# Passes 2 and 3 of a gated feed-forward: parting an odd chunk's activations beside the next chunk, and spreading the down weights' sums and loads over steps

## The chip, the cores and the metric

The kernel runs on one core of one Trainium2 chip. The metric is the device time of one launch in microseconds (us), as the median of several runs. The engines are named as in the profile: PE (TensorE, matmuls), PEld (its weight loads), ACT (ScalarE), DVE (VectorE), POOL (GpSimd), and SP, which here issues the DMAs. Each engine works through its own queue in order; semaphores tie the queues together.

## The reference

One transformer block in fp32 over 2048 tokens of width 1024, with a modulation (shift, scale, gate) computed from a condition vector `c`:

```python
x = A_x
sa, ca, ga, sb, cb, gb = silu(c) @ w_mod          # six rows of 1024
h = layernorm(x) * (1 + ca) + sa
x = x + ga * infini_attention(h)                  # 32 heads, 4 segments, with wq, wk, wv, wo
h = layernorm(x) * (1 + cb) + sb
x = x + gb * ((gelu(h @ w_gate) * (h @ w_up)) @ w_down)   # F = 3584
```

The change touches only the last line, the feed-forward.

## The kernel before

The attention and its projections come first (to about 1190 us of the profile). The feed-forward then runs in three passes over the tokens: 768, 640 and 640 of them (`PASSES`). Each pass walks over the 28 chunks of 128 columns of `w_gate`/`w_up` (`fc`; `m` counts chunks through all passes, so pass 2 begins at m = 28 and pass 3 at m = 56). The passes take the stretches 1190 to 1840, 1840 to 2415 and 2415 to 3012 us of the profile, roughly.

**Precision.** Each fp32 operand is parted into a high part (fp32r) and the rest: `cut`, or the local `put`, is one ACT copy for the high part (`nc.scalar.activation(hi, src, AF.Copy)`, L777 or L1082) and one subtraction for the low part (L779 on DVE for the down weights, L1083 on DVE for activations). Each product is three matmuls, hi·hi, lo·hi and hi·lo.

**One chunk** (`gate_up`, L1011 on) computes gate and up products with a seven-product (Winograd-Strassen) scheme. Seven products, in the order 1, 6, 2, 7, 5, 4, 3, go into three PSUM tiles `pa`, `pb`, `pc` (tile `f` in the profile, 12 matmuls each, all L1022). After product 1 ACT copies `pa` to `c1` (L1034, tile `c`); product 2 then goes on accumulating in `pa`, so it has to wait for this copy. After product 6 DVE forms `u2 = pb + c1` (L1036); product 7 then accumulates in `pb` and has to wait for that. Then come `g1 = gelu(pa)` (ACT L1038), two sums for `u3` (DVE L1040, L1042), `g2 = pb + c1` (DVE L1044), `g2 = gelu(g2)` (ACT L1045), and at the end `u2 += pc`, `g1 *= u2`, `g2 *= u3` (DVE L1047, L1048, L1049). The two results of a chunk are the tile `g`, of which there are two buffers.

**The down product** of passes 2 and 3 takes two chunks at a time, an even m and m + 1 (`down_seven`, matmuls L1148 into tiles `da`, `db`, `ds`, `dc`, `dd`). It is a seven-product scheme again, so it needs sums of both operands:

- `hidden(m)` makes the left operands (tile `hc`, three buffers). For an even chunk it parts `e1` and `e1 - e2`; for an odd chunk it needs sums with the even chunk before (`f`), and makes four parts: 512, 512, 256 and 128 columns wide. An odd chunk's `hidden` runs at the end of its `gate_up`; an even chunk's (but the first of a pass) is put into `delayed` and runs within the next `down_seven`, after the products `ds`.
- `t_part(m)` makes four of the right operands: it loads two raw chunks of `w_down` (tile `rt`, DMA at L1112), forms four differences on POOL (L790, two instructions of 256 columns each), and parts each into a tile `T` (ACT L777, DVE L779).
- `wd_load(m)` loads a chunk of `w_down` that pass 1 parted and stored in DRAM (tile `wd`, two buffers, 1 MB, DMA at L1010).

`gate_up`'s weights (tile `B`, eight buffers) are also loaded parted, seven products ahead (`b_load`, L978).

**The order.** PE's and SP's queues are in program order. For ACT, DVE and POOL a scheduler chooses the order from priorities; instructions handed to `keep` stay in program order among each other. `step()` is called after every half product, so 14 times in a chunk; it lets each generator in `sides` go on to its next `yield`. `flush` runs generators of a kind to their end.

The chunks of a pass follow each other as gate_up(odd m+1), gate_up(even m+2), down_seven(m), gate_up(odd m+3), and so on: from the second pair on, one period of the pass is two `gate_up` and one `down_seven`. The last two chunks of a pass (26 and 27) use a plain down product (`down`, L1211). The output of the pass is scaled and added to the residual beside the next pass (`finish`, L1284 and L1285).

## Time and profile before

| | us |
|---|---|
| median of 3 runs (lowest, highest) | 3024.54 (3022.23, 3025.67) |
| the profiled execution: its time | 3013.8 |
| the profiled execution: span from first to last instruction | 3012.1 |
| busy: PE / PEld | 2861.3 / 2551.1 |
| busy: DVE / ACT / POOL | 1884.0 / 1269.9 / 892.6 |
| mean granted TensorE clock | 0.983 |

The profiled execution was 10.7 us quicker than the median, so sums are made against 3013.8. The page gives busy times, a row per group of instructions and the chain of work that ended last; the trace also gives stretches of time ("windows"), the order of instructions in time with the idle time ahead of each and what ended it ("timeline"), and totals of who waited for whom ("waits"). An idle engine costs nothing unless PE, which is busy 95% of the span, waits for it.

### The profile page before, as it was taken

The page shows a single profiled execution, that of the slowest core. Times are in us where ns is not written, and L with a number is a line of the kernel's source. Part 1 is how long each engine was busy: PE and PEld are TensorE (multiplying, and loading weights), DVE is VectorE, ACT ScalarE, POOL GpSimd, SP SyncE. Part 2 cuts the span into 40 slices and gives each one's busy share as a digit, 9 for nine tenths or more (in the row PEclk, how much of TensorE's full clock was granted, in tenths as well). Part 3 has the DMA queues.
Part 4 walks back from the last instruction along what each step waited for, and adds up shares of the span by engine and source line. Part 5 has one row for each costly group of instructions (what it writes and reads, how often), then busy time and mean ns, then how long its engine had stood idle before and what let it go on. Part 6 is the DMA issues. An engine that isn't in the chain of part 4 may idle for free.

```text
span 3012.1 us, 48791 instructions
## 1 busy us (share of the span) xinstructions
PE 2861.3 (95%) x17248; PEld 2551.1 (85%) x17248; DVE 1884.0 (63%) x4289; ACT 1269.9 (42%) x3108; POOL 892.6 (30%) x1420
## 2 busy tenths in 40 slices
PE   6999999999999999999999999999999999999997
PEld 4788887888888778999999898888888888888987
DVE  7565657667567535666666667556556666556556
ACT  5777766766666443545323333211212231122111
POOL 0333334333334424534555441101111001111100
PEclk8999999999999999999999999999999999999999
DMA  7566657675556566888798887866777797777665
GB/s 238 102 137 140 143 107 139 148 134 113 109 103 133 151 213 222 320 321 308 280 357 304 293 307 286 345 246 249 263 267 264 252 346 263 262 259 272 250 243 192
DMA packets 233429, 684.02 MB, mean 227 GB/s; under 512 B 23392, under 2 KB 60256, under 8 KB 222432
## 3 DMA queue, kind: packets, MB, share of 16 engines
q1 hardware_dynamic: 233184, 680.90, 71.0%
q8 instruction: 136, 2.23, 0.3%
q14 instruction: 109, 0.89, 0.1%
HBM read 455.36 MB, written 175.11 MB: 209 GB/s over the span
## 4 chain that ended last, share of the span: by engine, by line
PE 61%; DVE 11%; DMA 11%; POOL 6%; ACT 5%; issue 5%; SPq 1%; DVEq 0%; POOLq 0%; ACTq 0%
PE f L1022 20%; PE kv L366 9%; PE d L1211 6%; DMA rt<-wd 5%; PE y L627 4%; PE q L372 3%; POOL rt L790 3%; PE T L557 3%; PE db L1148 2%; PE da L1148 2%; PE ds L1148 2%; PE dc L1148 2%; PE S L493 2%; PE O L566 2%; DVE T L779 1%
## 5 line engine op out<-in xcount | busy, mean ns | idle before, releaser
L1022 PE MATMUL f<-A,B 128*128 128x320 f32 (+1 forms) x7056 | 1149.4, 323 | 75.9 <-ACT c L1034 53.6
L1022 PEld LDWEIGHTS f<-A,B 128*128 128x128 f32 x7056 | 1126.0, 192 | 94.6 <-ACT c L1034 60.4
L495 DVE CUSTOM_DVE_ANT_0 sj<-S,mask 128x384 f32<-128x384 f32 (+3 forms) x512 | 229.6, 487 | 227.1 <-PE S L493 208.7
L790 POOL TENSOR_TENSOR rt<-rt 128x256 f32<-128x256 f32 x104 | 78.4, 774 | 948.4 <-DMA rt<-wd 882.8
L497 ACT ACTIVATE sj<-sj,mm 128x384 f32<-128x384 f32 (+3 forms) x512 | 281.4, 551 | 114.3 <-DVE mm L495 114.0
L560 POOL TENSOR_SCALAR_AFFINE_SELECT pt<-pt 128x128 f32<-128x128 f32 x512 | 170.8, 354 | 336.9 <-ACT pt L559 331.2
L1211 PE MATMUL d<-wd,hc 128*128 128x512 f32 x1128 | 259.8, 390 | 0.9 <-DVE hc L1074 0.7
L1211 PEld LDWEIGHTS d<-wd,hc 128*128 128x128 f32 x1128 | 211.1, 188 | 44.9 <-DVE hc L1074 1.0
L366 PE MATMUL kv<-w,hha 128*128 128x256 f32 x1024 | 206.7, 288 | 3.4 <-ACT hha L335 3.4
L366 PE MATMUL kv<-w,hhh 128*128 128x256 f32 x1024 | 201.6, 285 | 0.0
L559 ACT ACTIVATE pt<-T 128x256 f32<-128x256 f32 (+3 forms) x512 | 181.8, 457 | 37.3 <-PE T L557 33.4
L202 POOL TENSOR_TENSOR w<-r,w 128x256 fp32r<-128x256 f32 x180 | 133.3, 771 | 165.8 <-ACT w L197 165.8
L366 PEld LDWEIGHTS kv<-w,hha 128*128 128x128 f32 x1024 | 169.1, 194 | 4.7 <-ACT hha L335 4.3
L1082 ACT ACTIVATE hc<-g 128x256 fp32r<-128x256 f32 (+2 forms) x182 | 72.8, 440 | 227.5 <-DVE acc L1157 124.0
L366 PEld LDWEIGHTS kv<-w,hhh 128*128 128x128 f32 x1024 | 166.3, 191 | 0.3 <-issue 0.2
L1246 DVE TENSOR_TENSOR acc<-acc,d 128x512 f32<-128x512 f32 x176 | 118.2, 684 | 57.7 <-PE d L1211 56.2
L366 PE MATMUL kv<-w,hla 128*128 128x256 f32 x512 | 147.2, 288 | 6.0 <-DVE hla L336 4.2
L557 PEld LDWEIGHTS T<-qs,ks 128*128 128x128 f32 x512 | 80.6, 189 | 85.3 <-issue 35.1
L557 PE MATMUL T<-qs,ks 128*128 128x256 f32 (+2 forms) x512 | 128.6, 360 | 20.0 <-DVE qs L510 7.5
L1040 DVE TENSOR_TENSOR c<-f,c 128x320 f32<-128x320 f32 (+1 forms) x84 | 43.0, 511 | 167.0 <-PE f L1022 167.0
L366 PE MATMUL kv<-w,hlh 128*128 128x256 f32 x512 | 145.0, 283 | 0.0
L1045 ACT ACTIVATE g<-g 128x320 f32<-128x320 f32 (+1 forms) x84 | 41.0, 488 | 237.4 <-DVE g L1044 237.4
(240 smaller groups left out, 5270.5 us busy)
## 6 DMA issues: line engine op xcount, KB each, us to landing
B<-bc_d SPq DMA_DIRECT2D x392, 512.0 KB, 5.6
bc_d<-B SPq DMA_DIRECT2D x196, 512.0 KB, 6.3
wd<-wc_d SPq DMA_DIRECT2D x56, 1024.0 KB, 4.8
wc_d<-wd SPq DMA_DIRECT2D x28, 1024.0 KB, 8.0
rt<-wd SPq DMA_DIRECT2D x52, 512.0 KB, 7.3
ks<-kh SPq DMA_DIRECT2D x64, 256.0 KB, 5.6
qs<-qh SPq DMA_DIRECT2D x64, 256.0 KB, 7.4
wm<-wmod SPq DMA_DIRECT2D x32, 512.0 KB, 5.4
```

What stands on the lines that cost most here:

```text
L202: eng.tensor_sub(w[:, 1, k:k + 256], r[:, k:k + 256], f32(w[:, 0, k:k + 256]))
L366: nc.tensor.matmul(ps, b[:, sl], w[:, a], start=(kt == 0 and a == 0 and b is hi), stop=(kt == KT - 1 and a == 1), **kw)
L495: nc.vector.tensor_tensor_reduce(out=sj[:, :nv], in0=ps[:, :nv], in1=mask[:, L - nv:], scale=-1.0, scalar=3.4e38, op0=ALU.add, op1=ALU.min ...
L497: nc.scalar.activation(sj[:, :nv], sj[:, :nv], AF.Exp, bias=mm[:, j, i:i + 1], scale=-1.0, accum_out=ll[:, i, j:j + 1])
L557: nc.tensor.matmul(ps[:, :nn], ks[:, j, kc * P:(kc + 1) * P], qs[:, j, L - nn:], start=True, stop=True)
L559: nc.scalar.activation(pt, ps[:, nn - n:nn], AF.Exp)
L560: nc.gpsimd.affine_select(pt[:, :P], pt[:, :P], pattern=[[1, P]], compare_op=ALU.is_ge, fill=0.0, base=0, channel_multiplier=-1)
L627: nc.tensor.matmul(ps, b[:, i * P:(i + 1) * P], w[:, a, g % 2], start=(g == 0 and a == 0 and b is hi), stop=(g == G - 1 and a == 1))
L790: nc.gpsimd.tensor_sub(dst[:, k], a[:, k], b[:, k])
L1022: nc.tensor.matmul(ps, B[m, i][:, a, kt * P:(kt + 1) * P], A[p, i, kt][b], start=(start and kt == 0 and a == 0 and b == 0), stop=(kt == 3 ...
L1148: nc.tensor.matmul(ps, t[:, c:c + P], B(a), start=(start and a == 0 and b == 0), stop=(stop and a == 1), skip_group_check=True)
L1211: nc.tensor.matmul(ps, hid[m][:, b, tt * P:(tt + 1) * P], down_w[m][:, a, nb * L:(nb + 1) * L], start=(m == chunks[0] and a == 0 and b == ...
```

## The change

Five edits, all in the feed-forward of passes 2 and 3.

1. An odd chunk's `hidden` is no longer run at the end of its `gate_up`. It becomes a generator in `sides` that waits three steps of the next (even) chunk and then makes its four parts on four steps; `down_seven` is preceded by `flush("ht")`. Its instructions are marked `keep`.
2. Its sums change places: `s2 = e2 - f1` goes to a temporary tile, `e2` and `e1` are overwritten, so that the even chunk's tile `f` is only read at the start. Counts and widths of the parts stay (512, 256, 512, 128 columns).
3. The tile `g` of a chunk is taken after product 2 has been issued, not at the chunk's start, since its buffer is now read during the chunk.
4. `t_part` becomes `pair_part`: loads of `rt` on steps 0 and 1, differences on steps 6, 8, 10, 12, partings on steps 9, 13, 15, 17 (before: loads on step 0, differences on 8, 12, 16, 20, partings on 11, 15, 19, 23), and the two `wd` loads on steps 11 and 19 instead of straight behind `down_seven`.
5. In `finish`, the multiplication by the gate is marked `keep` as well.

```diff
@@ -1028,13 +1028,13 @@
 
             pa, pb, pc = (s_ps(f"f{q}_{m}")[:, :h] for q in range(3))
             c1, u2, u3 = (c_tile(f"c{q}_{m}")[:, :h] for q in range(3))
-            feat[m] = ffp[3].tile([P, 2, HM], F32, name=f"g{m}", tag="g", bufs=2)
-            g1, g2 = (feat[m][:, q, :h] for q in range(2))
             product(pa, 1, True)
             nc.scalar.activation(c1, pa, AF.Copy)
             product(pb, 6, True)
             nc.vector.tensor_add(u2, pb, c1)
             product(pa, 2, False)
+            feat[m] = ffp[3].tile([P, 2, HM], F32, name=f"g{m}", tag="g", bufs=2)
+            g1, g2 = (feat[m][:, q, :h] for q in range(2))
             nc.scalar.activation(g1, pa, AF.Gelu_apprx_tanh)
             product(pb, 7, False)
             nc.vector.tensor_add(u3, pb, c1)
@@ -1049,11 +1049,22 @@
             nc.vector.tensor_mul(g2, g2, u3)
             if p > 0 and fc % 2 == 0 and fc > 0:
 
-                delayed.append(lambda: hidden(m))
+                delayed.append(lambda: run(hidden(m)))
+            elif seven(m) and fc % 2:
+
+                sides.append([chain(wait_for(3), hidden(m, True)), 1, "h"])
             else:
-                hidden(m)
-
-        def hidden(m):
+                run(hidden(m))
+
+        def run(gen):
+            for _ in gen:
+                pass
+
+        def wait_for(n):
+            for _ in range(n):
+                yield
+
+        def hidden(m, behind=False):
 
 
             p, fc = divmod(m, FC)
@@ -1072,6 +1083,7 @@
                         hi, lo = (v.rearrange("p (q t) -> p q t", q=2) for v in (hi, lo))
                     nc.scalar.activation(hi, src, AF.Copy)
                     nc.vector.tensor_sub(lo, src, f32(hi))
+                    yield
                 return
 
             def put(t, at, n, src, q=1):
@@ -1079,9 +1091,9 @@
                 hi, lo = t[:, at:at + n], t[:, at + n:at + 2 * n]
                 if q == 2:
                     hi, lo = (v.rearrange("p (q t) -> p q t", q=2) for v in (hi, lo))
-                nc.scalar.activation(hi, src, AF.Copy)
-                nc.vector.tensor_sub(lo, src, f32(hi))
-
+                held(nc.scalar.activation(hi, src, AF.Copy), nc.vector.tensor_sub(lo, src, f32(hi)))
+
+            held = keep if behind else lambda *ins: None
             w = 2 * P
             e1, e2 = g[:, 0, :w], g[:, 1, :w]
             t = place(0).rearrange("p a b -> p (a b)")
@@ -1094,36 +1106,49 @@
                 return
             z = place(1).rearrange("p a b -> p (a b)")
             f = feat[m - 1]
-            nc.vector.tensor_add(f[:, 1, :w], f[:, 1, :w], e2)
-            nc.vector.tensor_sub(f[:, 0, :w], e2, f[:, 0, :w])
+            s2 = tmp_tile(f"s2_{m}")[:, :w]
             put(t, 0, 2 * w, g[:, :, :w], 2)
-            put(z, 0, 2 * w, f[:, :, :w], 2)
-            nc.vector.tensor_sub(e1, e1, f[:, 0, :w])
-            put(z, 4 * w, w, e1)
+            held(nc.vector.tensor_sub(s2, e2, f[:, 0, :w]))
+            held(nc.vector.tensor_add(e2, f[:, 1, :w], e2))
+            held(nc.vector.tensor_sub(e1, e1, s2))
+            yield
+            put(z, 0, w, s2)
+            yield
+            put(z, 2 * w, 2 * w, g[:, :, :w], 2)
+            yield
             put(t, 4 * w, P, g[:, :, w:h], 2)
-            left[m] = {2: (t, 0, 2 * w), 4: (t, w, 2 * w), 6: (z, 0, 2 * w), 5: (z, w, 2 * w), 3: (z, 4 * w, w),
+            left[m] = {2: (t, 0, 2 * w), 4: (t, w, 2 * w), 6: (z, 0, w), 3: (z, 2 * w, 2 * w), 5: (z, 3 * w, 2 * w),
                        0: (t, 4 * w, P)}
 
-        def t_part(m):
+        def pair_part(m):
+
 
             r = []
-            for q in range(2):
+
+            def raw(q):
                 r.append(ra_tile(f"rt{m + q}"))
                 nc.sync.dma_start(r[q], wd[(m + q) % FC])
-            b11, b12, b21, b22 = (r[q][:, k:k + L] for q in range(2) for k in (0, L))
-            for _ in range(8):
-                yield
+
+            def block(i, j):
+                return r[i][:, j * L:(j + 1) * L]
 
             def put(i, src):
                 t = big.tile([P, 2, L], F32R, name=f"T{m}_{i}", tag="raw", bufs=4)
-                cut(t[:, 0], t[:, 1], src, nc.vector)
+                cut(t[:, 0], t[:, 1], src, nc.vector, behind=True)
                 right[m, i] = t
 
-            for i, dst, a, b in ((5, b11, b12, b11), (7, b12, b22, b12), (6, b22, b22, b11), (4, b21, b21, b22)):
-                diff(dst, a, b)
-                for _ in range(3):
-                    yield
-                put(i, dst)
+            at = {11: lambda: wd_load(m), 19: lambda: wd_load(m + 1)}
+            if seven(m):
+                at.update({0: lambda: raw(0), 1: lambda: raw(1),
+                           6: lambda: diff(block(0, 0), block(0, 1), block(0, 0)),
+                           8: lambda: diff(block(0, 1), block(1, 1), block(0, 1)),
+                           10: lambda: diff(block(1, 1), block(1, 1), block(0, 0)),
+                           12: lambda: diff(block(1, 0), block(1, 0), block(1, 1)),
+                           9: lambda: put(5, block(0, 0)), 13: lambda: put(7, block(0, 1)),
+                           15: lambda: put(6, block(1, 1)), 17: lambda: put(4, block(1, 0))})
+            for n in range(24):
+                if n in at:
+                    at[n]()
                 yield
 
         def down_seven(m):
@@ -1281,7 +1306,7 @@
                 residual(q + 2)
                 yield
                 t = a[tt][:, nb * L:(nb + 1) * L]
-                nc.vector.tensor_mul(t, t, gbb[:, nb * L:(nb + 1) * L])
+                keep(nc.vector.tensor_mul(t, t, gbb[:, nb * L:(nb + 1) * L]))
                 keep(nc.vector.tensor_add(t, t, res[q]))
                 if nb:
                     later(4, lambda tt=tt: move_rows(p, tt, a[tt], out, store=True))
@@ -1318,25 +1343,21 @@
                 pend.append(m)
                 if len(pend) == 3:
                     if p > 0:
+                        flush("ht")
                         down_seven(pend[0])
                     else:
                         down(pend[:2], False)
                     pend = pend[2:]
                     if p > 0:
-                        wd_load(m)
-                        wd_load(m + 1)
-                        if seven(m):
-                            sides.append([t_part(m), 1])
-                        else:
+                        sides.append([pair_part(m), 1, "t"])
+                        if not seven(m):
                             sides.append([spread(), 1, "e"])
-            flush("e")
+            flush("et")
             down(pend, True)
             flush("a")
             send(True)
             if p + 1 < len(PASSES):
-                wd_load((p + 1) * FC)
-                wd_load((p + 1) * FC + 1)
-                sides.append([t_part((p + 1) * FC), 1])
+                sides.append([pair_part((p + 1) * FC), 1, "t"])
                 sides.append([finish(p), 1])
         yield
```

The instructions are the same in number and kind, and PE's queue is the same row by row. What moves is shown at three places, for the pair whose odd chunk is m = 43 and whose next even chunk is m = 44. In the names, `c_43` is a chunk's c1, u2 or u3, `f_43` its PSUM tiles; `g` and `hc` are followed by a running number only.

ACT's queue from chunk 43's gelu(pa) to chunk 44's, before:

```order
L1038 ACTIVATE g_24329<-f_43_24323 128x320
L777 ACTIVATE T_5_24425<-rt_24338 128x512
L777 ACTIVATE T_7_24483<-rt_24338 128x512
L777 ACTIVATE T_6_24518<-rt_24340 128x512
L777 ACTIVATE T_4_24553<-rt_24340 128x512
L1045 ACTIVATE g_24329<-g_24329 128x320
L1082 ACTIVATE hc_0_24449<-g_24329 128x512
L1082 ACTIVATE hc_1_24450<-g_24109 128x512
L1082 ACTIVATE hc_0_24449<-g_24329 128x128
L1034 ACTIVATE c_44_24465<-f_44_24462 128x320
L1082 ACTIVATE hc_1_24450<-g_24329 128x256
L1038 ACTIVATE g_24468<-f_44_24462 128x320
```

and now:

```order
L1038 ACTIVATE g_24380<-f_43_24326 128x320
L777 ACTIVATE T_5_24415<-rt_24340 128x512
L1045 ACTIVATE g_24380<-g_24380 128x320
L777 ACTIVATE T_7_24455<-rt_24340 128x512
L777 ACTIVATE T_6_24481<-rt_24348 128x512
L1032 ACTIVATE c_44_24464<-f_44_24461 128x320
L777 ACTIVATE T_4_24499<-rt_24348 128x512
L1094 ACTIVATE hc_0_24502<-g_24380 128x512
L1094 ACTIVATE hc_1_24503<-s_43_24504 128x256
L1038 ACTIVATE g_24531<-f_44_24461 128x320
```

The copy c1 of chunk 44 (`c_44<-f_44`) stood behind four T parts and three of chunk 43's four `hc` parts; now it stands behind three T parts and no `hc` part.

DVE's queue from chunk 43's `g2 = pb + c1` to chunk 44's u2, before:

```order
L1044 TENSOR_TENSOR g_24329<-f_43_24324,c_43_24326 128x320
L779 TENSOR_TENSOR T_4_24553<-rt_24340,T_4_24553 128x512
L1049 TENSOR_TENSOR g_24329<-g_24329,c_43_24328 128x320
L1097 TENSOR_TENSOR g_24109<-g_24109,g_24329 128x256
L1047 TENSOR_TENSOR c_43_24327<-f_43_24325,c_43_24327 128x320
L1098 TENSOR_TENSOR g_24109<-g_24329,g_24109 128x256
L1048 TENSOR_TENSOR g_24329<-g_24329,c_43_24327 128x320
L1083 TENSOR_TENSOR hc_0_24449<-g_24329,hc_0_24449 128x512
L1083 TENSOR_TENSOR hc_1_24450<-g_24109,hc_1_24450 128x512
L1101 TENSOR_TENSOR g_24329<-g_24329,g_24109 128x256
L1083 TENSOR_TENSOR hc_0_24449<-g_24329,hc_0_24449 128x128
L1036 TENSOR_TENSOR c_44_24466<-f_44_24463,c_44_24465 128x320
```

and now:

```order
L1044 TENSOR_TENSOR g_24380<-f_43_24327,c_43_24329 128x320
L1049 TENSOR_TENSOR g_24380<-g_24380,c_43_24331 128x320
L779 TENSOR_TENSOR T_7_24455<-rt_24340,T_7_24455 128x512
L1047 TENSOR_TENSOR c_43_24330<-f_43_24328,c_43_24330 128x320
L779 TENSOR_TENSOR T_6_24481<-rt_24348,T_6_24481 128x512
L1048 TENSOR_TENSOR g_24380<-g_24380,c_43_24330 128x320
L779 TENSOR_TENSOR T_4_24499<-rt_24348,T_4_24499 128x512
L1094 TENSOR_TENSOR hc_0_24502<-g_24380,hc_0_24502 128x512
L1111 TENSOR_TENSOR s_43_24504<-g_24380,g_24171 128x256
L1034 TENSOR_TENSOR c_44_24465<-f_44_24462,c_44_24464 128x320
```

Chunk 44's u2 (`c_44<-f_44,c_44`) had the first sums and parts of chunk 43 ahead of it; now three T parts, the first `hc` part and `s2` stand between chunk 43's g2 and it, and the other sums and parts of chunk 43 follow it.

SP's queue from the B load behind which `down_seven` is issued, before:

```order
L978 DMA B_3_24214<-bc_d 128x1024
L1010 DMA wd_24319<-wc_d 128x2048
L1010 DMA wd_24321<-wc_d 128x2048
L978 DMA B_1_24330<-bc_d 128x1024
L1112 DMA rt_24338<-wd 128x1024
L1112 DMA rt_24340<-wd 128x1024
L978 DMA B_6_24349<-bc_d 128x1024
```

and now:

```order
L978 DMA B_3_24221<-bc_d 128x1024
L978 DMA B_1_24332<-bc_d 128x1024
L1130 DMA rt_24340<-wd 128x1024
L1130 DMA rt_24348<-wd 128x1024
L978 DMA B_6_24351<-bc_d 128x1024
L978 DMA B_2_24366<-bc_d 128x1024
L978 DMA B_7_24382<-bc_d 128x1024
L978 DMA B_5_24399<-bc_d 128x1024
L978 DMA B_4_24419<-bc_d 128x1024
L1010 DMA wd_24435<-wc_d 128x2048
L978 DMA B_3_24439<-bc_d 128x1024
```

The two `wd` loads stood ahead of the `rt` loads; now the `rt` loads come right behind one B load, the first `wd` load stands behind five more B loads, and the second one five places behind that. (The new kernel's line numbers are shifted by 2 or more: L1034 stands now for u2 and L1032 for c1, L1094 for the `hc` parts, L1130 for the `rt` loads.)

## The prediction

> **What bounds the kernel now.** First the page:

> ```profile
> span 3012.1 us, 48791 instructions
> PE 2861.3 (95%) x17248; PEld 2551.1 (85%) x17248; DVE 1884.0 (63%) x4289; ACT 1269.9 (42%) x3108; POOL 892.6 (30%) x1420
> ```

> PE sets the end, so what can be won is time in which PE idles or has a lower clock. The windows of the three passes show where:

> ```profile
> 1190.00:1840.00 650.00, 642.02 (x3411) 599.31 (x3410) 430.29 (x669) 265.33 (x515) 313.45 (x368) 1.00 0.83 304
> 1840.00:2415.00 575.00, 541.27 (x3121) 500.78 (x3120) 350.84 (x654) 122.39 (x266) 86.31 (x104) 0.98 0.75 275
> 2415.00:3012.00 597.00, 547.85 (x3145) 507.85 (x3143) 359.36 (x666) 117.10 (x253) 84.34 (x104) 0.96 0.72 260
> ```

> Columns: stretch, length, busy time (count) of PE, PEld, DVE, ACT, POOL, granted clock, DMA share, GB/s. Pass 1 has PE busy for 642 of 650 us at clock 1.00. Passes 2 and 3 leave it idle for 34 and 49 us, at 0.98 and 0.96. PE's group and its waits in 1840 to 3012 us say for whom:

> ```profile
> L1022 PE MATMUL f<-A,B 128*128 128x320 f32 x4704 | 732.8, 317 | 68.8 <-ACT c L1034 53.5 <-DMA B<-bc_d 6.1 <-DVE c L1036 5.3
> PE f L1022 <- ACT c L1034: 53.5, 24, 3.3
> PE f L1022 <- DVE c L1036: 5.3, 2, 2.7
> PE f L1022 <- DVE c L1042: 3.3, 6, 0.8
> ```

> Of 68.8 us, 53.5 are 24 waits for one instruction, c1 (ACT, L1034), which product 2 needs. One of them in the timelines of PE, ACT and DVE (start, duration, engine, line, operation, count, idle time before and its releaser):

> ```profile
> 2026.95 16.00 PE L1022 MATMUL f<-A,B 128*128 128x320 f32 x108
> 2045.23 9.06 PE L1022 MATMUL f<-A,B 128*128 128x320 f32 x60 [2.28 <-ACT c L1034]
> ```
> ```profile
> 2028.97 0.44 ACT L1034 ACTIVATE c<-f 128x320 f32<-128x320 f32 x1 [7.21 <-PE f L1022]
> 2042.98 0.48 DVE L1048 TENSOR_TENSOR g<-g,c 128x320 f32<-128x320 f32 x1
> 2043.50 1.35 ACT L1082 ACTIVATE hc<-g 128x512 fp32r<-128x512 f32 x3 [2.15 <-DVE g L1048]
> 2044.76 0.41 ACT L1034 ACTIVATE c<-f 128x320 f32<-128x320 f32 x1
> ```

> The 108 matmuls are the odd chunk's 84 and the even chunk's products 1 and 6. At 16.00/108 = 0.148 us each, a product takes 1.78 us. The odd chunk's c1 started 2.02 us after its first matmul. The even chunk's first matmul is at 2026.95 + 84 × 0.148 = 2039.4, so its c1 could have run from 2041.4 to 2041.9, 1.1 us before PE ended product 6 at 2042.95. It ran at 2044.76 instead, since three `hc` parts of the odd chunk stood ahead of it on ACT and waited for DVE's L1048.

> The stall has a second cost. The rest of the even chunk behind it is 60 matmuls in 23 of the 24 cases. The one above took 9.06 us, as did seven others; 15 took over 10.3. The first, a usual one and the last of these 15:

> ```profile
> 2004.19 10.40 PE L1022 MATMUL f<-A,B 128*128 128x320 f32 x60 [2.45 <-ACT c L1034]
> 2085.00 10.59 PE L1022 MATMUL f<-A,B 128*128 128x320 f32 x60 [2.35 <-ACT c L1034]
> 2948.90 10.60 PE L1022 MATMUL f<-A,B 128*128 128x320 f32 x60 [2.20 <-ACT c L1034]
> ```

> 10.59 - 9.06 = 1.53 us for the same matmuls: lower clock right after an idle gap, 15 × 1.53 = 23 us in all, which fits clocks of 0.98 and 0.96 beside pass 1's 1.00.

> **The change, part by part.**

> *Odd chunks' parts move (edits 1 and 2).* Counts and widths stay, so ACT and DVE have no more work. On ACT c1 of the even chunk stands ahead of every `hc` part, so this wait goes: minus 53.5 us, and minus 23 us of clock. What is late next is u2 (DVE, L1036), which product 7 needs. Its chain is worked out from these rows:

> ```profile
> 2039.92 0.63 ACT L777 ACTIVATE T<-rt 128x512 fp32r<-128x512 f32 x1 [0.77 <-POOL rt L790]
> 2040.36 0.48 DVE L1044 TENSOR_TENSOR g<-f,c 128x320 f32<-128x320 f32 x1
> 2040.76 0.68 DVE L779 TENSOR_TENSOR T<-rt,T 128x512 fp32r<-128x512 f32 x1
> 2040.88 0.47 ACT L1045 ACTIVATE g<-g 128x320 f32<-128x320 f32 x1 [0.32 <-DVE g L1044]
> 2041.38 0.49 DVE L1049 TENSOR_TENSOR g<-g,c 128x320 f32<-128x320 f32 x1
> 2042.65 0.42 DVE L1098 TENSOR_TENSOR g<-g,g 128x256 f32<-128x256 f32 x1
> 2044.16 1.29 DVE L1083 TENSOR_TENSOR hc<-g,hc 128x512 fp32r<-128x512 f32 x2 [0.70 <-ACT hc L1082]
> ```

> On the same clock: the odd chunk's product 4 ends after 72 matmuls, at 2037.6, so L1044 runs to 2038.2, the gelu to 2038.7, L1049 to 2039.2. T 7 on ACT to 2039.3, on DVE to 2040.0; L1047 (as L1044) to 2040.5; T 6 to 2041.2; L1048 to 2041.7. T 4 on ACT follows c1, 2041.9 to 2042.5, on DVE to 2043.2; the 512-wide `hc` part, half of 1.29, to 2043.8; `s2` (as L1098) to 2044.3; u2 to 2044.7. Product 7 is due at 2042.95 + 1.78 = 2044.7. Its cover is gone, then, but just so. Rows that follow each other overlap by some 0.08 us (2040.36 + 0.48 against 2040.76), which lowers the sum; a hand-over raises it. I take 0.1 us for 24 pairs, plus 2 us; bounds are 0 and, with T parts as slow as below, 1.7 us a pair. Six waits for L1042, which stood behind T parts, go: minus 3 us.

> *The tile g later (edit 3)* costs nothing unless gelu(pa) waits for the odd chunk's sums; ACT runs it some 0.4 us later, and PE does not need its PSUM tile again within the chunk.

> *rt, T and wd (edit 4).* SP stood in the `wd` loads before, POOL got `rt` late, and differences and T parts ran side by side:

> ```profile
> 2019.49 6.57 SPq L1010 DMA_DIRECT2D wd<-wc_d  x2
> 2026.64 1.11 SPq L1112 DMA_DIRECT2D rt<-wd  x2
> 2033.37 1.44 POOL L790 TENSOR_TENSOR rt<-rt 128x256 f32<-128x256 f32 x2 [34.51 <-DMA rt<-wd]
> 2034.76 3.73 POOL L790 TENSOR_TENSOR rt<-rt,rt 128x256 f32<-128x256 f32 x4
> 2038.45 1.44 POOL L790 TENSOR_TENSOR rt<-rt 128x256 f32<-128x256 f32 x2
> 2039.19 1.25 DVE L779 TENSOR_TENSOR T<-rt,T 128x512 fp32r<-128x512 f32 x1 [1.29 <-ACT T L777]
> ```

> Now nothing that waits for the down product stands ahead of `rt`. The B load before it can go once its buffer is free, at about the start of the down product (2014), so `rt` may come up to 12 us earlier, POOL is done by about 2029, and T parts cost DVE 0.68 us and not 1.25. The `wd` loads get B loads ahead of and behind them. Landing times, 1900 to 2400 us:

> ```profile
> wd<-wc_d SPq DMA_DIRECT2D x25, 1024.0 KB, 4.8
> rt<-wd SPq DMA_DIRECT2D x24, 512.0 KB, 7.3
> 2984.17 13.79 PE L1211 MATMUL d<-wd,hc 128*128 128x512 f32 x60
> ```

> The second `wd` load goes out when the even chunk's product 6 is done. Five products (8.9 us) and 15 matmuls of the down product (13.79/60 = 0.23 us each, 3.4 us) lie before its first use: 12 us of cover for 4.8. Only at the end of a pass is it short: the load for chunk 27 goes out with that chunk's last product, 1.8 us before `down`, whose first 18 matmuls (4.1 us) use the other chunk: 5.9 us for a landing of 4.8 to 7.3, so 0 to 1.4 us, twice; I take 2 us in all. For the start of a pass, where the order of `finish` changes too (edit 5), I take nothing, with 5 us either way, the size of the L1036 waits there.

> **Sum** against the profiled 3013.8: - 53.5 - 23 - 3 + 2 + 2 = - 75.5, so 2938. The median was 10.7 us above the profiled run; carried over, 2949.

> **The rivals.**

> *The wait moves to u2.* For it speaks that its cover is used up. If `rt` comes no earlier, three T parts cost 0.57 us more each, 1.7 us a pair. Half of that, 0.9 × 24 = 21 us, and a few low clocks, give 2970 to 2990.

> *The clock does not come back.* Eight of 23 stalls, of the same length, were followed by full clock, so the gap alone does not decide. If the low stretches have another cause, 23 us stay: 2972. Against it: every one of the 15 begins at a stall, and pass 1, with PE denser, ran at 1.00. [...]

> *POOL beside the down product.* With `rt` early, POOL's differences fall where DVE adds up the down products:

> ```profile
> 2022.36 0.68 DVE L1157 TENSOR_TENSOR acc<-acc,dc 128x512 f32<-128x512 f32 x1
> 2024.17 1.54 PE L1148 MATMUL dc<-wd,hc 128*128 128x512 f32 x6
> ```

> The second of the two tiles `dc` is read by 2023.0, and PE goes on in it three matmuls after 2024.17, at 2024.9: 1.9 us of slack. Ahead of that read DVE has four instructions of an even chunk's `hidden`. If each waits for one POOL instruction (1.44/2 = 0.72 us), that is 2.9 us, 1.0 us of stall in a pair, 24 us: 2973. [...]

> *Slower: POOL's differences come late.* T 4 waits for POOL's last difference, and T 4 (0.63 and 1.25), the `hc` part, `s2` and u2 follow it: 3.4 us. From the landing of `rt` to that difference it was 6.5 us (2033.4 to 2039.9). So u2 ends 9.9 us after the landing, and is due at 2044.7. A pair now loses 76.5/24 = 3.2 us, of which 1.0 is clock. From a stall of 2.2 us on, a landing at 2037, 3.7 us later than before, it is a loss; 1 us beyond, 24 us: 3049. Against it: SP has less ahead of `rt` than before. If the landing falls just at that point, or c1 waits behind T 6 as long as it did behind `hc`, the change does not do what it says and nothing moves: 3024.

> **How the numbers follow.** Forecast, 2935 to 2962: 0.66. Wait at u2: 0.12. Clock stays: 0.10. POOL beside the down product: 0.05. Nothing moves: 0.03. Slower: 0.04. A measurement of this kernel can tell about 0.2% (6 us) from no change, so faster 0.93, same 0.03, slower 0.04. The range begins at 2932: if the median's extra 10.7 us were clock lost at the other eight stalls (8 × 1.53 = 12 us), it goes too, and the start of a pass may give 5. It ends at 2980, so as to take in the rivals at 2972 and 2973 and half of the wait at u2.

> **What would show it.** In the changed profile the waits of PE for c1 should be gone from the 24 places, and 168 matmuls of a pair should run in one piece of some 25 us, followed by a down product. The clock of passes 2 and 3 should be 0.99 or more, their PE idle time together below 35 us instead of 83. POOL's wait for `rt` should end some 10 us earlier relative to the odd chunk's first matmul, and T parts on DVE should cost 0.68 us. A row "PE f <- DVE c" for u2 of over 10 us would be the first rival; PE waits at `dc` the third; waits for `wd` ahead of `down`, the price at the ends of passes. The prediction would be wrong outright if PE waited for T, `wd` or `rt` in every pair.

## The result, and the profile after

The changed kernel takes 2942.78 us (median of 4 runs, 2937.51 to 2944.91), the kernel before 3024.01 us (median of 4 runs). The ratio is 0.9729, with a 95% interval of 0.9712 to 0.9746. The forecast was 2949 us in a range of 2932 to 2980. The profiled execution took 2937.51 us against 3013.8, which is 76.3 us less; the sum of the prediction had 75.5 less.

The head of the page of the changed kernel:

```profile
span 2935.8 us, 48789 instructions
PE 2833.2 (97%) x17248; PEld 2530.0 (86%) x17248; DVE 1854.5 (63%) x4289; ACT 1259.7 (43%) x3108; POOL 869.4 (30%) x1420
```

PE went from 95% to 97% of a shorter span. Two sets of windows of the changed kernel follow, with the same columns as before (stretch, length, busy time and count of PE, PEld, DVE, ACT, POOL, clock, DMA share, GB/s): first passes 2 and 3, then their steady parts and the stretch between them.

```profile
1840.00:2380.00 540.00, 525.10 (x3112) 488.11 (x3111) 340.44 (x669) 122.54 (x279) 73.71 (x104) 0.99 0.80 300
2380.00:2936.00 556.00, 536.95 (x3168) 500.51 (x3166) 340.84 (x657) 107.99 (x243) 73.41 (x104) 0.98 0.74 274
```
```profile
1930.00:2350.00 420.00, 420.00 (x2496) 391.83 (x2495) 261.87 (x512) 83.48 (x190) 61.98 (x88) 1.00 0.75 282
2350.00:2440.00 90.00, 74.17 (x421) 68.81 (x420) 57.35 (x115) 23.40 (x56) 5.61 (x8) 0.91 0.82 302
2440.00:2860.00 420.00, 420.00 (x2497) 391.88 (x2496) 256.93 (x503) 88.28 (x199) 66.64 (x95) 1.00 0.76 284
```

Read the second set first. In the pairs PE is busy for 420.00 of 420 us at clock 1.00: nothing is left to win there by order. What is lost is lost between the passes, 2350 to 2440, where PE is busy for 74 of 90 us at a clock of 0.91. The group of the gate and up products and the waits of PE in 1840 to 2936 us name the rest:

```profile
L1022 PE MATMUL f<-A,B 128*128 128x320 f32 x4704 | 699.6, 310 | 11.5 <-DVE c L1034 5.6 <-DMA B<-bc_d 2.4 <-DVE c L1042 2.2
```
```profile
PE d L1236 <- DMA wd<-wc_d: 7.7, 1, 7.7
PE f L1022 <- DVE c L1034: 5.6, 2, 4.7
PE f L1022 <- DVE c L1042: 2.2, 1, 2.2
```

The 24 waits for c1 (53.5 us before) are gone, and no row for u2 (now L1034) has taken their place: its 5.6 us are two waits at the starts of the passes. The matmuls themselves shrank too, from 317 to 310 ns on average. A new row stands on top: `down` (now L1236) waited once for `wd`, for 7.7 us.

A pair in the timeline of PE of the changed kernel, with the start of the next one:

```profile
2018.09 24.80 PE L1022 MATMUL f<-A,B 128*128 128x320 f32 x168
2055.25 24.80 PE L1022 MATMUL f<-A,B 128*128 128x320 f32 x168
```

All 168 matmuls run in one piece, and a pair takes 37.16 us. Before, a pair had 108 and 60 matmuls with a gap between.

**Where the time went.** By start times in the two timelines of PE: from the first `da` of pass 2 to the start of the last odd chunk's products it was 500.8 us and is 459.1 us (-41.7). In pass 3 it was 503.5 and is 458.5 (-45.0). The start of pass 2 gives another 4.1. The stretch from the last odd chunk of pass 2 to the first `da` of pass 3 went from 73.0 to 84.6 (+11.6). Pass 2's gate and up products began 2.9 later (1850.15 against 1847.22); that start varies from run to run, between 1845.5 and 1856.9 in three executions of kernels that are the same up to there. Together: -41.7 - 45.0 - 4.1 + 11.6 + 2.9 = -76.3. So the pairs gave 86.7 us, more than the sum had for everything, and the end of pass 2 took some back.

Here is that end in the changed kernel, first SP's queue (L840 loads the next pass's activations, L1010 is `wd`), then PE:

```profile
2357.46 2.16 SPq L840 DMA_DIRECT2D ra<-mix_d  x2
...
2366.68 0.36 SPq L840 DMA_DIRECT2D ra<-mix_d  x1
2367.28 0.33 SPq L1010 DMA_DIRECT2D wd<-wc_d  x1
...
2369.07 0.32 SPq L1010 DMA_DIRECT2D wd<-wc_d  x1
```
```profile
2362.85 2.02 PE L1022 MATMUL f<-A,B 128*128 128x320 f32 x12 [1.19 <-DVE c L1040]
2367.11 2.03 PE L1022 MATMUL f<-A,B 128*128 128x320 f32 x12 [2.23 <-DVE c L1042]
2376.84 16.54 PE L1236 MATMUL d<-wd,hc 128*128 128x512 f32 x60 [7.71 <-DMA wd<-wc_d]
2393.22 17.76 PE L1022 MATMUL f<-A,B 128*128 128x320 f32 x120
2415.67 21.58 PE L1022 MATMUL f<-A,B 128*128 128x320 f32 x132 [4.70 <-DVE c L1034]
```

The two `wd` loads of the last pair stand on steps 11 and 19 now. That puts them in SP's queue behind the loads of the next pass's activations, which held it until 2367. They were issued at 2367.28 and 2369.07, when the last chunk's products were nearly done: the first one 14.75 us after that chunk's first matmul (2352.53), where in the pair shown above it goes out 9.36 us after it (2027.45 against 2018.09). And it landed only 9.5 us later, at 2376.8, beside other loads (DMA share 1.0). So `down` had to wait 7.71 us. It then ran its 60 matmuls in 16.54 us; the same 60 took 13.79 before. In the kernel before both loads had gone out ahead of those activations, straight behind the last `down_seven`:

```profile
2387.93 6.57 SPq L1010 DMA_DIRECT2D wd<-wc_d  x2
```

Pass 3 has no pass behind it, and there `down` followed without a wait.

### The profile page after: what moved, and what is told of

Its sections match the earlier page's. It is cut to its first block, busy times and chain, and to the rows that moved or that the text cites. A ratio compares the mean times of both kernels' runs of the same rounds, so it can differ in the third digit from the quotient of the medians.

```text
span 2935.8 us, 48789 instructions
## 1 busy us (share of the span) xinstructions
PE 2833.2 (97%) x17248; PEld 2530.0 (86%) x17248; DVE 1854.5 (63%) x4289; ACT 1259.7 (43%) x3108; POOL 869.4 (30%) x1420
## 4 chain that ended last, share of the span: by engine, by line
PE 76%; DVE 8%; DMA 6%; ACT 4%; issue 3%; POOL 3%; SPq 0%; DVEq 0%; POOLq 0%; ACTq 0%
PE f L1022 32%; PE kv L366 9%; PE d L1236 7%; PE y L627 4%; PE q L372 3%; PE T L557 3%; PE dc L1173 2%; PE db L1173 2%; PE ds L1173 2%; PE da L1173 2%; PE S L493 2%; PE O L566 2%; ACT sj L497 2%; PE dd L1173 1%; DVE qs L510 1%
## 5 line engine op out<-in xcount | busy, mean ns | idle before, releaser
L1022 PE MATMUL f<-A,B 128*128 128x320 f32 (+1 forms) x7056 | 1116.3, 318 | 17.9 <-DVE c L1034 11.1
L1022 PEld LDWEIGHTS f<-A,B 128*128 128x128 f32 x7056 | 1101.7, 188 | 27.8 <-DVE c L1034 14.5
L790 POOL TENSOR_TENSOR rt<-rt 128x256 f32<-128x256 f32 x104 | 75.7, 750 | 888.1 <-DMA rt<-wd 607.9
L1236 PE MATMUL d<-wd,hc 128*128 128x512 f32 x1128 | 262.6, 393 | 8.8 <-DMA wd<-wc_d 7.7
L1236 PEld LDWEIGHTS d<-wd,hc 128*128 128x128 f32 x1128 | 212.9, 189 | 53.7 <-DMA wd<-wc_d 8.0
L1045 ACT ACTIVATE g<-g 128x320 f32<-128x320 f32 (+1 forms) x84 | 41.1, 489 | 299.2 <-DVE g L1044 299.2
L1032 ACT ACTIVATE c<-f 128x320 f32<-128x320 f32 (+1 forms) x84 | 38.3, 456 | 268.7 <-PE f L1022 268.7
L1094 ACT ACTIVATE hc<-g 128x256 fp32r<-128x256 f32 (+1 forms) x156 | 64.5, 446 | 154.2 <-DVE acc L1182 124.0
## 6 DMA issues: line engine op xcount, KB each, us to landing
B<-bc_d SPq DMA_DIRECT2D x392, 512.0 KB, 6.8
bc_d<-B SPq DMA_DIRECT2D x196, 512.0 KB, 6.4
wd<-wc_d SPq DMA_DIRECT2D x56, 1024.0 KB, 8.3
wc_d<-wd SPq DMA_DIRECT2D x28, 1024.0 KB, 8.1
rt<-wd SPq DMA_DIRECT2D x52, 512.0 KB, 8.2
wm<-wmod SPq DMA_DIRECT2D x32, 512.0 KB, 5.4
```

The costliest lines, as they stand in the source:

```text
L1022: nc.tensor.matmul(ps, B[m, i][:, a, kt * P:(kt + 1) * P], A[p, i, kt][b], start=(start and kt == 0 and a == 0 and b == 0), stop=(kt == 3 ...
L1236: nc.tensor.matmul(ps, hid[m][:, b, tt * P:(tt + 1) * P], down_w[m][:, a, nb * L:(nb + 1) * L], start=(m == chunks[0] and a == 0 and b == ...
```

## The experiments

All runs are kernels on one core. Each batch has its own median of the kernel before: 3025.37 us for the first four, 3021.37 for the next four, 3023.6 for the last two.

**Edits 1 to 3 and 5 without edit 4.** The odd chunk's parts move, the loads and T parts stay as before (excerpt):

```diff
-sides.append([pair_part(m), 1, "t"])
+wd_load(m); wd_load(m + 1)
+if seven(m): sides.append([t_part(m), 1])
```

> Edits 1 to 3 and 5 alone; t_part and the wd loads as before. Theory (the wait for c1 behind the odd chunk's parts, and the clock it costs, are the whole gain): the waits of PE for c1 are gone, u2 comes some 0.2 to 0.3 us late in each of 24 pairs (about 6 us), and the wait for wd at the end of pass 2 is absent; 2930 to 2950 us, so no slower than the full change. Rival (the early rt loads of edit 4 are needed, since u2 becomes the bound without them): waits for u2 of 1 us and more in each pair, 2970 to 2990 us.

2954.42 us, ratio 0.9768 (0.9751 to 0.9784): 4 us above the theory's range and well below the rival's. The waits for c1 are gone, and PE's waits and a pair look like this:

```profile
PE f L1022 <- DVE c L1034: 13.2, 14, 3.9
PE f L1022 <- DVE c L1042: 3.5, 5, 1.0
```
```profile
2062.88 25.14 PE L1022 MATMUL f<-A,B 128*128 128x320 f32 x168
```

So edits 1 to 3 bring most of the gain by themselves. Twelve pairs, from odd chunk to odd chunk, take 454.96 us here in pass 2 and 456.13 in pass 3, and 445.92 in either with edit 4. So a pair is 0.8 us longer, 19 us in both passes: u2 is late in most pairs, and in a few a sum for u3 (L1042). That is close to the price that the prediction's first rival had given for slow T parts (0.9 us). The T parts in both kernels (shortest/median/longest, ns), this one first, then the full change:

```profile
L779 DVE TENSOR_TENSOR T<-rt,T x104: 674/828/1258, 1868.4 to 2888.1; 128x512 fp32r<-128x512 f32 x104
```
```profile
L779 DVE TENSOR_TENSOR T<-rt,T x104: 680/689/1111, 1859.5 to 2873.7; 128x512 fp32r<-128x512 f32 x104
```

With edit 4 the typical T part costs 0.69 us, and u2 is on time, as the prediction counted on. Why it does so is asked further below.

**Edit 4 alone.** `pair_part` in the kernel before, the odd chunk's parts at the end of its `gate_up` (excerpt, seen from the changed kernel):

```diff
-sides.append([chain(wait_for(3), hidden(m, True)), 1, "h"])
+hidden(m)
```

> Edit 4 alone; the odd chunk's parts stay at the end of its gate_up. Theory: u2 of the even chunk still stands behind all parts of the odd chunk on DVE, ending near 19.5 us after the odd chunk's first matmul where it is due at 17.6, so a stall of about 2 us a pair stays, at u2 in place of c1, with its clock; with the wait at the end of pass 2 on top 3005 to 3040 us. Rival (the T parts and the wd loads were what held c1 up): 2940 to 2965 us.

2977.67 us, ratio 0.9842 (0.9828 to 0.9857): between the two numbers. On ACT c1 ran ahead of the `hc` parts here without being moved, and PE now waited for u2 (here L1036), behind the odd chunk's sums on DVE:

```profile
PE f L1022 <- DVE c L1036: 35.4, 26, 1.7
```
```profile
2045.37 7.30 PE L1022 MATMUL f<-A,B 128*128 128x320 f32 x48 [1.39 <-DVE c L1036]
```

All 24 gaps in the pairs are of 1.39 us, and all 24 runs of 48 matmuls behind them take 7.30 or 7.31 us: no low clock. Alone, the halves bring 71 us (edits 1 to 3 and 5) and 48 us (edit 4), together 81: in part they take away the same loss, so their gains don't add up. The 7.30 us also shows a price of a gap by itself: at 24.80/168 = 0.1476 us each, 48 matmuls in one piece take 7.09. Starting again costs some 0.2 us, which the prediction didn't count. By the length of a pair it is 0.26: 38.81 us here against 37.16 without the gap of 1.39.

**The last pair's wd loads early.** The full change, but the two loads of the last pair of a pass go on steps 0 and 1:

```diff
-at = {11: lambda: wd_load(m), 19: lambda: wd_load(m + 1)}
+at = ({11: lambda: wd_load(m), 19: lambda: wd_load(m + 1)} if seven(m)
+      else {0: lambda: wd_load(m), 1: lambda: wd_load(m + 1)})
```

> The full change, but the two wd loads for the last two chunks of a pass go out on steps 0 and 1 and not on 11 and 19. Theory (the second wd load stands behind the next pass's A loads on SP and lands 8 us late): the wait of 7.7 us ahead of down goes, and with it part of the low clock there (0.91 over 90 us); 2926 to 2936 us. Rival (the A loads then come late, or DVE's queue at the boundary holds PE anyway): 2938 to 2945 us.

2924.19 us, ratio 0.9668 (0.9649 to 0.9687), 2 us below the theory's range. The same window between the passes, then the loads and `down` in the timelines:

```profile
2350.00:2440.00 90.00, 84.61 (x484) 76.78 (x483) 65.92 (x131) 29.89 (x68) 6.09 (x8) 1.00 0.93 348
```
```profile
2360.74 0.90 SPq L1010 DMA_DIRECT2D wd<-wc_d  x2
```
```profile
2372.61 13.79 PE L1236 MATMUL d<-wd,hc 128*128 128x512 f32 x60
...
2404.91 12.59 PE L1022 MATMUL f<-A,B 128*128 128x320 f32 x84 [0.92 <-DVE c L1034]
```

The wait for `wd` is gone, `down` is back at 13.79 us, and the clock at 1.00. From the start of the last odd chunk's products to the first `da` of pass 3 it is now 70.0 us, against 84.6 with the full change: 14.6 us. That is more than the wait and its low clock (7.7 + 2.75). The waits for the last chunk's sums (L1040, L1042) shrank from 3.4 us to 0.2, and that for u2 at the start of pass 3 from 4.7 to 0.9. The first two have a visible cause on DVE, where parts of the next pass's activations (`A<-ra`, L779) ran among the last chunk's sums. In the full change six such parts stood straight ahead of L1040, and two that had waited 2.15 us for ACT stood ahead of L1042; here it was four, and none. Why the wait for u2 shrank was not traced. In return PE waited here for `B` and `g` ahead of that `da`, 4.3 us in all, where it had not with the full change.

**All wd loads as before, the rest new.** Both loads straight behind every `down_seven`:

```diff
-at = {11: lambda: wd_load(m), 19: lambda: wd_load(m + 1)}
+at = {}
...
+wd_load(m); wd_load(m + 1)
 sides.append([pair_part(m), 1, "t"])
```

> The full change, but all wd loads straight behind the down product as before, so that rt comes late again and T parts run beside POOL's differences. Theory (early rt gives u2 its cover of 0.3 us): T parts on DVE take about 1 us in place of 0.69, u2 waits of 0.3 to 0.9 us in each pair, 7 to 22 us, against 8 to 14 us won at the end of pass 2: 2936 to 2956 us. Rival (the place of rt does not matter to PE): no waits for u2 in the pairs, 2926 to 2936 us.

2939.68 us, ratio 0.9716 (0.9701 to 0.9732), which can't be told from the full change. It lies in the theory's range, but the waits for u2 that the theory rests on did not come. The waits of PE:

```profile
PE f L1022 <- DMA B<-bc_d: 7.2, 6, 1.9
PE f L1022 <- DVE c L1034: 5.9, 2, 3.3
PE f L1022 <- DVE c L1042: 4.6, 7, 0.9
```

POOL and the T parts, whose rows follow, show what the `wd` loads do to a pair that starts at 2027.46:

```profile
2033.75 1.43 POOL L790 TENSOR_TENSOR rt<-rt 128x256 f32<-128x256 f32 x2 [30.53 <-DMA rt<-wd]
```
```profile
L779 DVE TENSOR_TENSOR T<-rt,T x104: 674/692/1250, 1870.7 to 2878.1; 128x512 fp32r<-128x512 f32 x104
```

`rt` is as late as in the kernel before: POOL starts 6.3 us after the odd chunk's first matmul (6.4 before). Yet this pair takes 37.16 us, no listed wait in the pairs is for u2, and most T parts cost 0.69 us. So an early `rt` is not what keeps u2 on time, but the rest of edit 4, the steps and the kept order of differences and T parts. The early `rt` pays in another way. A T part that runs beside POOL still takes 1.25 us here, and in six of the 24 pairs L1042 stood behind one and PE waited for it:

```profile
1999.05 1.24 DVE L779 TENSOR_TENSOR T<-rt,T 128x512 fp32r<-128x512 f32 x1 [2.11 <-ACT T L777]
2000.22 0.48 DVE L1042 TENSOR_TENSOR c<-f,c 128x320 f32<-128x320 f32 x1
```
```profile
2000.75 14.35 PE L1022 MATMUL f<-A,B 128*128 128x320 f32 x96 [0.82 <-DVE c L1042]
```

All pairs together take 5.9 us more than with the full change. From its first matmul of the gate and up products to its first `da`, pass 2 takes 46.75 us against 43.25, another 3.5. The stretch at the end of pass 2 is 9.8 us shorter (74.8 against 84.6). So moving the `wd` loads paid about as much as it cost at the end of pass 2, which is why the two kernels can't be told apart.

**A gap of one's own making.** To see what a gap does to the clock, u2 of each even chunk was computed four times, and then six times, in the kernel with the early `wd` loads:

```diff
-nc.vector.tensor_add(u2, pb, c1)
+for _ in range(4 if m > FC and fc % 2 == 0 else 1):
+    nc.vector.tensor_add(u2, pb, c1)
```

> e3_wd_last_early with u2 of each even chunk of passes 2 and 3 (the first of pass 2 excepted) computed four times over on DVE, so that product 7 waits for it: a gap of about 0.5 + 3 × 0.41 = 1.7 us a pair and nothing else new on PE. Theory (it is the length of a gap that lowers the clock; 1.4 us did not in e2, 2.2 us did in two of three pairs): 24 gaps of 1.7 us, 41 us, and a lower clock behind some of them: 2965 to 2978 us. Rival (the low clock of the kernel before had another cause than the gap): clock 1.00 in the pairs, 2965 us.

> The same with u2 computed six times: a gap of about 0.5 + 5 × 0.41 = 2.5 us a pair. Theory: 60 us of gaps, and 1.5 us of low clock behind at least two of three of them, 24 to 37 us: 3008 to 3022 us. Rival: no low clock, 2984 us.

Four times: 2999.22 us, ratio 0.992 (0.9889 to 0.995), 21 us above the theory's range. Six times: 3023.01 us, ratio 1.0003 (0.9988 to 1.0018), 1 us above the theory's range and 39 us above the rival's number. Two of the gaps in each kernel, of four times and of six:

```profile
2088.08 7.31 PE L1022 MATMUL f<-A,B 128*128 128x320 f32 x48 [1.77 <-DVE c L1035]
...
2246.41 8.84 PE L1022 MATMUL f<-A,B 128*128 128x320 f32 x48 [1.77 <-DVE c L1035]
```
```profile
2017.44 10.04 PE L1022 MATMUL f<-A,B 128*128 128x320 f32 x48 [2.82 <-DVE c L1035]
...
2270.27 7.30 PE L1022 MATMUL f<-A,B 128*128 128x320 f32 x48 [2.82 <-DVE c L1035]
```

All gaps of a kernel have the same length; what follows has not. Of 24 gaps of 1.77 us, 7 were followed by 7.30 or 7.31 us and 17 by 8.83 to 8.85, 1.53 us more. Of 24 gaps of 2.82 us, 5 were followed by 7.30 to 7.32, 15 by 8.72 to 8.85, and 4 by 9.96 to 10.07. The 24 gaps of 1.39 us cost no clock, and in the kernel before 15 of 22 gaps of 2.13 to 3.31 us did. The clock over 1930 to 2340 and 2440 to 2850 us is 0.98 and 0.96 with four times and 0.95 and 0.96 with six, against 1.00 in both without the gaps. This makes the low clock a consequence of gaps as short as 1.77 us. Their length alone does not decide; what went with it in the traces is shown in the last section. The cost of a stall was then its length, 0.2 us to start again, and in most cases 1.5 us of clock. For four times that is 24 × (1.77 + 0.2) + 17 × 1.53 = 73 us, for six times 24 × (2.82 + 0.2) + 15 × 1.5 + 4 × 2.7 = 106 us. In the traces, from the first `da` of each pass to its last, they take 74.9 and 107.1 us more than the kernel without gaps. (The medians differ by 75 and 99 us; the profiled execution of six times was the slowest of its runs, 15 us above its median.) So the mechanism held, and its size was set too small for the shorter gap.

**Two small parts.** The kernel with early `wd` loads, once without edit 5, once with the loads of a pass's first pair on steps 0 and 1 as well (the second edit is shortened):

```diff
-keep(nc.vector.tensor_mul(t, t, gbb[:, nb * L:(nb + 1) * L]))
+nc.vector.tensor_mul(t, t, gbb[:, nb * L:(nb + 1) * L])
```

> e3_wd_last_early without edit 5, so that the multiplications of finish are again free to move. Theory (edit 5 matters only at the start of a pass, where DVE is full): the waits of PE for c1, u2 and B within 60 us of a pass start change by 0 to 5 us in all, either way: 2919 to 2930 us. Rival (edit 5 is what keeps u2 in time at the start of a pass): over 2930 us.

```diff
-... if seven(m) else {0: lambda: wd_load(m), 1: lambda: wd_load(m + 1)}
+... if seven(m) and m % FC else {0: lambda: wd_load(m), 1: lambda: wd_load(m + 1)}
```

> e3_wd_last_early with the two wd loads of a pass's first pair on steps 0 and 1 as well, ahead of the residual loads of finish on SP. Theory (B loads late at the start of a pass, 6.0 us of PE's waits, come from SP's queue being full of finish's loads and stores that wait for DVE, not from the wd loads): nothing won, 2921 to 2930 us. Rival (the two wd loads among them make B late): up to 6 us faster, 2915 to 2921 us.

2924.26 us (0.9676, 0.9645 to 0.9707) and 2929.66 us (0.9693, 0.9664 to 0.9721). Edit 5 makes no difference that these runs can tell. Nor do earlier loads at the start of a pass win anything: PE waited 7.8 us for `B` there, against 6.0 without them.

**Side by side.** The full change and the version with early last loads, once more on one chip, five rounds each:

> The full change once more, beside the next kernel on one chip, for a ratio between the two: 0.973 of the kernel before, as measured.

> The kernel of e3 on the same chip as e9. Theory (the late wd loads at the end of pass 2 and the low clock behind them cost the full change some 16 to 20 us): 0.967 of the kernel before, 0.993 to 0.995 of e9. Rival (the difference of e3 was one between chips): within 0.2% of e9.

2938.32 us (0.9719, 0.9703 to 0.9735) and 2923.7 us (0.9676, 0.9658 to 0.9694). The difference of 14.6 us is the one seen between the passes. This version beats both kernels.

## Why the prediction was right, and where its terms were off

The forecast held, and its total came close to the profiled difference in part because errors of opposite sign met.

- **c1, minus 53.5 us: right.** Its row is gone, and the pairs have no gap. The run with edit 4 alone adds what the prediction did not see: that half takes the waits for c1 away too, and leaves 35.4 us of waits for u2, where there were 5.3.
- **Clock, minus 23 us: right in kind, too small.** The busy time of the L1022 group fell by 33.2 us (732.8 to 699.6). The working took 9.06 us for 60 matmuls as undisturbed. In one piece they take 60 × 0.1476 = 8.86, so each of 24 gaps had also cost 0.2 us, 5 us together. Some 3 us more were two low stretches at the starts of the passes, outside the 15 counted. The "eight of 23 stalls, of the same length" at full clock were not all of that length: one was of 0.78 us and one of 3.22, and one of the 15 low runs took 11.55 us, not 10.6. The sum of 23 us is not changed by this. The rival that the clock would stay is refuted: windows of the pairs show 1.00, and the runs with gaps put back brought the low clock back (0.95 to 0.98).
- **L1042, minus 3 us: right in the pairs.** One wait of 2.2 us is left, at the end of pass 2, where the prediction had not looked.
- **u2, plus 2 us: it was 0 in the pairs.** The working had it at 2044.7, 17.75 us after the odd chunk's first matmul at 2026.95. In the changed kernel's timeline of DVE it ends 17.4 us after that matmul (2018.09):

```profile
2033.41 0.69 DVE L779 TENSOR_TENSOR T<-rt,T 128x512 fp32r<-128x512 f32 x1 [0.92 <-ACT T L777]
2034.02 0.69 DVE L1094 TENSOR_TENSOR hc<-g,hc 128x512 fp32r<-128x512 f32 x1
2034.62 0.42 DVE L1111 TENSOR_TENSOR s<-g,g 128x256 f32<-128x256 f32 x1
2034.96 0.49 DVE L1034 TENSOR_TENSOR c<-f,c 128x320 f32<-128x320 f32 x1
```

  Rows that follow each other overlap by 0.08 to 0.15 us (2034.02 + 0.69 against 2034.62), which the text had named and left out of the sum. Product 7 begins after 120 matmuls, at 2018.09 + 120 × 0.1476 = 2035.8; u2 ends at 2035.45. The slack is 0.35 us, so the cover is as thin as the prediction said, but it holds.
- **`rt` and T parts: right in what is seen, wrong in part in why.** T parts cost 0.69 us, and `rt` is early, but the first is due to the second only in part: with all `wd` loads as before `rt` was late, and most T parts cost 0.69 us all the same. What the early `rt` saved was 5.9 us in the pairs, most of it waits for L1042; u2 is on time without it. POOL's first two differences began 6.4 us after the odd chunk's first matmul before (2033.37 against 2026.95), and begin 4.4 us ahead of it now, 10.8 us earlier:

```profile
2043.34 1.80 SPq L1130 DMA_DIRECT2D rt<-wd  x2
```
```profile
2050.89 1.44 POOL L790 TENSOR_TENSOR rt<-rt 128x256 f32<-128x256 f32 x2 [31.64 <-DMA rt<-wd]
```

  They fall beside the down product, as the third rival had it. But the instructions of the even chunk's `hidden`, which that rival took to be slowed, had ended here by 2050.74, just before POOL began. DVE's sums beside POOL did not slow down (two in 1.28 us at that very time, one in 0.68 just before), so the wait of 0.72 us for each instruction that its sum took is not shown here, and no wait in the pairs names `dc`. That rival is refuted, and the slower one, with POOL late, never came near.

```profile
2051.25 1.28 DVE L1182 TENSOR_TENSOR acc<-acc,da 128x512 f32<-128x512 f32 x2
```

- **wd at the ends of passes, plus 2 us: the term that was mis-sized.** The prediction took 5.9 us of cover for a landing of 4.8 to 7.3 us, "so 0 to 1.4 us, twice". It counted from the step at which the load is issued, and did not list what stands ahead of it in SP's queue at that place: the loads of the next pass's activations. It also looked only at chunk 27's load. The one that `down` waited for was chunk 26's, which the prediction took to be in place: issued at 2367.28, it took 9.5 us to land. That cost 7.7 us of wait and 2.75 us of clock in one place, and 14.6 us with all that hung on it; at the end of pass 3, without such loads ahead, it cost nothing.
- **Starts of passes, 0 with 5 either way:** about -4 us at pass 2; at pass 3 it can't be told apart from the late `wd`.
- **The signs:** PE's idle time in the windows of both passes is 14.9 + 19.1 = 34.0 us, just below the 35 named. The clock reached 1.00 in the pairs, but 0.98 over pass 3, since the end of pass 2 weighs on it.
- **Median and profile:** the 10.7 us between the median and the profiled run were carried over whole. The medians differ by 81.2 us, the profiled runs by 76.3, so half of it went. The prediction had named clock lost at the stalls as a possible cause; no run tested it. Another is the part ahead of pass 2, whose end varied by 11.4 us between executions.

## What to carry to other kernels

When a load is moved to a later step, write down everything that its queue holds ahead of it at each place where the step occurs, the rare places (the last pair of a pass) above all: there two 1 MB loads behind other loads took back 15 of 100 us. When a wait goes, work out the next one from row to row, overlaps included, since 0.35 us decided here between no wait and one in every pair. And price a stall of PE above its length: here 0.2 us to start again, and 1.5 us or more of clock after 17 of 24 gaps of 1.77 us and 19 of 24 of 2.82. The 24 gaps of 1.39 us were free of that second price.

## What was not expected of the hardware

Gaps of one length had two outcomes: after 1.77 us PE ran 48 matmuls in 7.31 us in 7 of 24 cases and in 8.84 in the others, in runs of like outcome (the five from 2009.69 to 2166.48 full, the next five low). After 2.82 us a third outcome came up, 10.0 us. After 1.39 us there was only the first.

```profile
2123.23:2126.64 3.41, 1.26 (x8) 1.00 (x8) 2.71 (x7) 1.67 (x4) 0.00 (x0) 1.00 0.89 264
2126.64:2130.05 3.41, 3.41 (x15) 3.41 (x14) 0.96 (x4) 0.85 (x2) 0.00 (x0) 0.50 0.23 94
```
```profile
2205.15:2208.56 3.41, 1.62 (x12) 1.35 (x10) 2.66 (x6) 1.01 (x3) 0.00 (x0) 1.00 0.89 314
2208.57:2211.97 3.40, 1.98 (x13) 1.98 (x14) 2.57 (x6) 1.79 (x5) 0.00 (x0) 1.00 0.50 164
```

The first gap lies in one step as a whole, and the next step runs at 0.50. The second, though longer, is cut by a border between two steps into 1.80 and 1.42 us, and the clock stays at 1.00. From pass 2 to the last matmul, in these two traces, a step at full clock in which PE was idle for 1.95 us or more was followed by a low one in 18 of 18 cases, and a step with 1.79 us or less in none; in between, one with 1.82 us was and one with 1.89 us was not. The gaps of 1.77 us, which had both outcomes, lie at the edge of that, and those of 1.39 us below it. A low step was followed by another one in the four cases where 1.18 us or more of idle time lay in it, and by full clock in the 19 with 0.52 us or less. Behind the gap of 3.31 us in the kernel before lay two low steps (2577.20 to 2584.03), and 60 matmuls took 11.55 us there. That the 10.0 us come from two low steps as well is an estimate from that case.
